# Second products by seven half-size products, for chunks 2 and 3 of the first block and for the second block

## The chip, the cores and the metric

The kernel runs on one core of a Trainium2 chip. The metric is the device time of one execution in microseconds; the median of three runs of the kernel before is 205.09 us (204.23 to 205.53). A second, profiled execution gives the trace that the text reads.

## What is computed

A retention layer (linear attention with a decay per head), then a feed-forward layer with a squared relu. Four batches of 768 tokens, 8 heads of 64, so x has 3072 rows of 512; the feed-forward layer goes 512 to 2048 to 512.

```
state = gamma[h] * state + outer(k[t], v[t])     # per batch and head, over t
y[t]  = q[t] @ state / sqrt(64)
x     = y, heads side by side                    # 3072 x 512
h     = maximum(x @ w_in, 0)                     # 3072 x 2048, "first products"
out   = (h * h) @ w_out                          # 3072 x 512,  "second products"
```

## The kernel before

**Chunks and blocks.** The 3072 tokens are 24 chunks of 128. `BLOCKS` puts four chunks in the first block and two in each of ten others. The feed-forward layer works block by block; the attention of later chunks is threaded between its pieces, so that TensorE always has work.

**Pieces and places.** The order of each engine is written out by hand. `ffn_pieces(tb)` is a generator that issues one piece of a block's feed-forward work per step; after each piece a counter n goes up and `before(n)` issues what `put(place, ...)` has registered for that place, and then the squares that are due. Engines take their instructions in that order and wait only for data and buffers. The first block has pieces 5 to 16 (first products of 12 of the 16 rows of blocks of h; four are done earlier) and 17 to 32 (second products). The second block has pieces 33 to 40 (first products, one per chunk and quarter) and 41 to 48 (second products); the third 49 to 56 and 57 to 64. Attention steps of chunk m are registered by `attend` (chunks 4 to 7) and `attend2` (from 8): scaling of q, k and v, transposes, scores with a mask, state, outputs.

**First products** (L826): `w_in` is the stationary operand, x the moving one; ScalarE takes the relu (L835), VectorE, or ScalarE where so marked, the square in place (L804, L806).

**Second products, plain** (L1022): for a chunk of 128 tokens, 16 matmuls of 512 columns, h the stationary operand, `w_out` the moving one. ScalarE copies the sum out (L1032), SP stores it (L1034). In the first block the four chunks go together, a quarter g of `w_out` at a time: four matmuls per piece, each quarter of `w_out` used by four pieces.

**Second products, seven half products** (L860, in blocks that `SEVEN` names, from the third on): two chunks of tokens, the even and odd blocks of h, and the two halves of the output columns make 2x2 matrices, which are multiplied with seven products instead of eight (Winograd's form of Strassen's scheme). Each product is 8 matmuls of 256 columns. VectorE makes four sums of h (`s1` = a21 + a22, `s2` = s1 - a11, `s3` = a11 - a21 in place of a21, `s4` = a12 - s2; `first_sums` makes the first two in halves) and, after the products, `u`, `v` and three output sums with operands in PSUM (all L856). The four differences of `w_out` (`t1` to `t4`, `sum_w_out`, L319) are made once, for the two halves of `w_out` apart. The last product is put off into the next block (`kept`).

**Buffers and queues.** The first and second products share four PSUM buffers (`ps_f`); the transposes use one (`ps_tp`), the scores one (`ps_st`). `spare` is a tile of the pool of h that the prologue uses for scores. The second half of `w_out`'s quarters come by GpSimd's DMA queue (`load_w_out`, L170, places 6, 8, 11, 14, with a cast on the way); all other loads and the stores are issued by SP in order. `cast_k2` (L688) and the copies of L705 are GpSimd's work for chunks from 8 on, `transpose_k2` (L711) a DMA transpose of what L688 wrote. `pack_constants` and `zero_off_diagonal` (L358) prepare constants and zeros for that later form of attention.

## Time and profile before

| | us |
|---|---|
| median of three runs | 205.09 |
| the profiled execution, its own time | 204.37 |
| its span, first to last instruction | 202.5 |
| granted TensorE clock over the span | 1.00 |
| second products of the first block begin | 30.92 |
| first products of the second block begin | 47.63 |
| first products of the third block begin | 65.29 |
| second products of the third block begin | 73.58 |
| a later block of two chunks, start to start (104.78 to 119.74) | 14.96 |

Times inside the span are counted from its start. A row of the table of groups reads: line, engine, operation, written tile from read tiles, shapes, number of instructions; then busy time in total and the mean of one in ns; then the idle time of the engine just before them and what ended it. A row of a timeline reads: start, length, engine, line, operation, and in brackets the idle time before it and who ended that. Matmuls of a run overlap in the pipeline, so the length of a run divided by its number is less than the duration that one matmul shows.

The engines over three later stretches, one of them in the steady state (columns: stretch, its length, then busy time and number of instructions of PE, PEld, DVE, ACT and POOL, granted clock, DMA share, GB/s):

```profile
43.00:48.00 5.00, 4.95 (x51) 3.31 (x51) 3.84 (x7) 4.08 (x8) 0.61 (x1) 1.00 1.09 267
73.60:80.50 6.90, 6.88 (x103) 6.08 (x100) 5.81 (x11) 4.11 (x10) 2.32 (x4) 1.00 0.76 140
104.60:119.60 15.00, 15.00 (x190) 13.57 (x188) 12.34 (x25) 10.45 (x22) 5.50 (x8) 1.00 0.97 203
```

### The profile page before, as it was taken

The page shows a single profiled execution, that of the slowest core. Times are in us where ns is not written, and L with a number is a line of the kernel's source. Part 1 is how long each engine was busy: PE and PEld are TensorE (multiplying, and loading weights), DVE is VectorE, ACT ScalarE, POOL GpSimd, SP SyncE. Part 2 cuts the span into 40 slices and gives each one's busy share as a digit, 9 for nine tenths or more (in the row PEclk, how much of TensorE's full clock was granted, in tenths as well). Part 3 has the DMA queues.
Part 4 walks back from the last instruction along what each step waited for, and adds up shares of the span by engine and source line. Part 5 has one row for each costly group of instructions (what it writes and reads, how often), then busy time and mean ns, then how long its engine had stood idle before and what let it go on. Part 6 is the DMA issues. An engine that isn't in the chain of part 4 may idle for free.

```text
span 202.5 us, 5744 instructions
## 1 busy us (share of the span) xinstructions
PE 195.7 (97%) x2321; PEld 160.1 (79%) x2327; DVE 151.2 (75%) x309; ACT 127.6 (63%) x258; POOL 68.0 (34%) x131
## 2 busy tenths in 40 slices
PE   5899999999999999999999999999999999999993
PEld 1478444558965998988989999999889899999883
DVE  3986768268597888788798798798797797485374
ACT  8764872348853766782784785783775776763730
POOL 8693711311330552282225225252225225100000
PEclk9999999999999999999999999999999999999999
DMA  5999999999979478979979998979998254300202
GB/s 169 356 375 398 338 195 197 260 233 320 236 160 262 125 159 156 202 204 223 171 214 164 214 208 203 226 182 227 212 157 200 107 105 49 111 3 0 107 0 104
DMA packets 92250, 38.12 MB, mean 188 GB/s; under 512 B 68544, under 2 KB 88256, under 8 KB 92224
## 3 DMA queue, kind: packets, MB, share of 16 engines
q1 hardware_dynamic: 90112, 35.66, 72.3%
q0 software_dynamic: 2112, 2.10, 6.2%
q8 instruction: 18, 0.29, 0.6%
q14 instruction: 8, 0.07, 0.1%
HBM read 27.26 MB, written 6.29 MB: 166 GB/s over the span
## 4 chain that ended last, share of the span: by engine, by line
PE 89%; DVE 4%; DMA 2%; ACT 2%; issue 1%; DVEq 0%
PE psf L826 40%; PE psf L860 18%; PE psf L1022 10%; PE tp L860 7%; DMA qn<-in_q_dram 2%; PE y L783 2%; PE st L727 2%; PE y L776 2%; PE c_ps L754 2%; DVE h L806 1%; PE c_ps L627 1%; PE st L430 1%; PE y L506 1%; ACT h L835 1%; PE y L342 1%
## 5 line engine op out<-in xcount | busy, mean ns | idle before, releaser
L826 PE MATMUL psf<-xt,w_in_bf 128*128 128x256 bf16 (+2 forms) x879 | 92.2, 259 | 0.2 <-issue 0.2
L826 PEld LDWEIGHTS <-w_in_bf 128*128 128x128 bf16 x880 | 71.2, 98 | 11.4
L835 ACT ACTIVATE h<-psf 128x512 bf16<-128x512 f32 x96 | 56.1, 594 | 20.1 <-PE psf L826 18.5
L806 DVE TENSOR_TENSOR h<-h 128x512 bf16<-128x512 bf16 x80 | 35.6, 460 | 19.2 <-ACT h L835 18.8
L688 POOL CAST ks_bdp<-stage 64x512 bf16<-64x512 f32 x32 | 24.5, 767 | 38.7 <-issue 30.7
L705 POOL COPY v_bd<-v 64x512 bf16<-64x512 bf16 x32 | 20.6, 643 | 42.0 <-DVE v L697 36.7
L860 PEld LDWEIGHTS <-h 128*128 128x128 bf16 x288 | 26.3, 98 | 3.8 <-DVE h L806 1.0
L1022 PE MATMUL psf<-w_out_bf,h 128*128 128x512 bf16 x91 | 21.9, 379 | 0.4 <-issue 0.2
L860 PE MATMUL tp<-w_out_bf,h 128*128 128x256 bf16 x136 | 19.4, 273 | 0.2 <-DVE h L806 0.2
L860 PE MATMUL psf<-w_sum,h 128*128 128x256 bf16 x136 | 19.1, 273 | 0.0
L860 PE MATMUL psf<-w_sum,k_bd 128*128 128x256 bf16 x144 | 17.9, 273 | 0.0
L361 DVE TENSOR_TENSOR qs<-qn,qf 128x512 bf16<-128x512 f32 x20 | 16.3, 824 | 0.0
L1022 PEld LDWEIGHTS <-h 128*128 128x128 bf16 x96 | 8.9, 98 | 9.0
L860 PEld LDWEIGHTS <-k_bd 128*128 128x128 bf16 x144 | 13.7, 98 | 1.5
L763 ACT ACTIVATE s_bd<-c_ps 64x256 bf16<-64x256 f32 x29 | 10.7, 370 | 6.5 <-PE c_ps L754 6.5
L856 DVE TENSOR_TENSOR osb<-psf,u 128x256 f32<-128x256 f32 x26 | 10.3, 421 | 6.1 <-PE psf L860 5.8
L856 DVE TENSOR_TENSOR u<-psf,u 128x256 f32<-128x256 f32 x18 | 7.6, 423 | 8.9 <-PE psf L860 8.7
L697 DVE TENSOR_TENSOR v<-stage,kf 128x512 bf16<-128x512 f32 x16 | 12.5, 783 | 0.0
L764 ACT ACTIVATE s_bd<-c_ps 64x256 bf16<-64x256 f32 x29 | 11.0, 378 | 0.4
L734 DVE TENSOR_TENSOR pt<-st,cmask 128x512 bf16<-128x512 f32 x16 | 11.0, 687 | 0.1
L856 DVE TENSOR_TENSOR k_bd<-h 128x512 bf16<-128x512 bf16 x18 | 10.7, 597 | 0.3
L896 ACT ACTIVATE osb<-tp 128x256 f32<-128x256 f32 x8 | 3.1, 384 | 12.2 <-PE tp L860 12.2
(133 smaller groups left out, 262.4 us busy)
## 6 DMA issues: line engine op xcount, KB each, us to landing
qn<-in_q_dram SPq DMA_DIRECT2D x12, 512.0 KB, 4.9
out_dram<-osb SPq DMA_DIRECT2D x23, 256.0 KB, 2.4
stage<-in_k_dram SPq DMA_DIRECT2D x32, 96.0 KB, 3.4
stage<-in_v_dram SPq DMA_DIRECT2D x32, 96.0 KB, 3.5
stage<-in_moe_w_in_dram SPq DMA_DIRECT2D x4, 512.0 KB, 7.1
stage<-in_moe_w_in_dram SPq DMA_DIRECT2D x2, 1024.0 KB, 10.2
w_out_bf<-in_moe_w_out_dram POOLq DMA_DIRECT2D x4, 512.0 KB, 10.3
kn<-in_k_dram SPq DMA_DIRECT2D x6, 256.0 KB, 6.0
```

The lines of the kernel that those rows point to most:

```text
L361: engine.tensor_tensor(out=out, in0=by, in1=table[:, :, None].to_broadcast([P, H, D]), op=ALU.mult)
L688: nc.gpsimd.tensor_copy(ks[rows, :, hh, :].rearrange("s (u p) d -> s u p d", u=2), kn[rows])
L697: nc.vector.tensor_tensor(out=v2.rearrange("s (u p) d -> s u p d", u=2), in0=vn, in1=kf2[:, i, :, :, None].to_broadcast([P, 2, NPAIR, D]), ...
L705: nc.gpsimd.tensor_copy(v_bd[rows, :, hh, :], v2[rows])
L734: nc.vector.tensor_tensor(out=pt[:], in0=st[:], in1=cmask2.rearrange("s r t -> s (r t)")[:, None, :].to_broadcast([P, 2 * NPAIR, C // 2]), ...
L764: nc.scalar.activation(s_bd[halves[1], :, 1, :], c[halves[1]], AF.Copy)
L806: nc.vector.tensor_mul(hv, hv, hv)
L826: nc.tensor.matmul(hp, lhsT=w_in_bf[g][:, cb, fq * 128 : (fq + 1) * 128], rhs=xts[tb][:, cb, cols], start=(cb == 0), stop=(cb == NCB - 1),)
L835: nc.scalar.activation(hv, hp[:], AF.Relu)
L856: nc.vector.tensor_tensor(out=out, in0=in0, in1=in1, op=op)
L860: nc.tensor.matmul(to, lhsT=left[:, j], rhs=right(j) if callable(right) else right[:, j], start=(start and j == 0), stop=(stop and j == NF ...
L1022: nc.tensor.matmul(op[:], lhsT=h_of(tb, f)[:, 0, j * C : (j + 1) * C], rhs=w_out_bf[g][:, fq, cols], start=(f == 0), stop=(f == NFB - 1),)
```

## The change

Chunks 2 and 3 of the first block, and the second block, get their second products as seven half products. Chunks 0 and 1 keep the plain form.

In the first block the 16 pieces of second products are rewritten (`last_of_first`). Pieces 17 to 22, 25 and 26 each hold two of the 16 steps of chunks 0 and 1 together (four matmuls of 512) and one matmul of 256 of the half product `pa`; a quarter of `w_out` is so used up by two pieces. The other pieces hold the remaining products in halves, the last one is put off into piece 34. `pa` and `pe` share one PSUM buffer, `pd` and `pb` another. The sums `s1`, `s2` and `s4` lie in `spare`; `first_sums` are issued at places 11 and 17, `s3` and `s4` at 22.

In the second block `SEVEN` now applies. Its `s1`, `s2` and `s4` get a tile of the pool of h; `s4` is made on GpSimd.

Around it: the differences of `w_out` move from places 25, 31 and 48 to 20, 23 and 27; chunk 4's scaling of q from 21 to 13 and 15, its other steps up to four places earlier; chunks 5 and 7 move by up to three places; the transposed k of chunk 7 uses the scores' PSUM buffer. Three things leave VectorE: the zeros of `zero_off_diagonal` and the scaling of q for chunk 8 go to GpSimd, and the square of one piece of the second block goes to ScalarE.

```diff
-SEVEN = range(2, 11)
+SEVEN = range(1, 11)
...
     def zero_off_diagonal(t, hh):
-        nc.vector.memset(t[halves[hh], :, 1 - hh, :], 0.0)
+        nc.gpsimd.memset(t[halves[hh], :, 1 - hh, :], 0.0)
...
+        if tb == 1:
+            room = hpool.tile([P, 4096], BF16, name="h2").rearrange("e (n j t) -> e n j t", n=4, t=C)
+            s1, s2, s4 = (room[:, n] for n in range(3))
...
-            add(s4, a12, s2, ALU.subtract)
+            add(s4, a12, s2, ALU.subtract, nc.gpsimd if tb == 1 else nc.vector)
...
+    def last_of_first():
...
+        def first_sums(x):
+            add(s1[x], a21[x], a22[x])
+            add(s2[x], s1[x], a11[x], ALU.subtract)
+
+        def last_sums():
+            for x in range(2):
+                add(s3[x], a11[x], a21[x], ALU.subtract)
+            for x in range(2):
+                add(s4[x], a12[x], s2[x], ALU.subtract)
+
+        def second_products():
+            ops = [ps_f.tile([P, DM], FP32, name="psf") for _ in range(2)]
+            pa, pe, pd, pb = (
+                t[:, n * HN : (n + 1) * HN]
+                for t in [ps_f.tile([P, DM], FP32, name="psf") for _ in range(2)]
+                for n in range(2)
+            )
...
+            def plain(j):
+                for f in (2 * j, 2 * j + 1):
+                    for c, op in enumerate(ops):
+                        nc.tensor.matmul(
+                            op[:],
+                            lhsT=h_of(0, f)[:, 0, c * C : (c + 1) * C],
+                            rhs=w_out_bf[f // FPQ][:, f % FPQ, :],
+                            start=(f == 0),
+                            stop=(f == NFB - 1),
+                        )
+                product(pa, a11, b(0, 0), (j,))
+
+            lo, hi = range(0, 4), range(4, 8)
+            for j in range(6):
+                plain(j)
+                yield
+            product(pd, s1, t1, lo)
+            product(pb, s2, t2, lo, False)
+            yield
+            product(pe, a22, t4, lo, False)
+            yield
+            plain(6)
+            yield
+            plain(7)
+            nc.scalar.activation(a[:], pa, AF.Copy)
+            for c, op in enumerate(ops):
+                osb = opool.tile([P, DM], FP32, name="osb")
+                nc.scalar.activation(osb[:], op[:], AF.Copy)
+                nc.sync.dma_start(out[c * C : (c + 1) * C], osb[:])
+            yield
+            product(pa, a12, b(1, 0), lo, False)
+            product(pa, a12, b(1, 0), hi, False)
+            nc.scalar.activation(oa[:, 0:HN], pa, AF.Copy)
+            yield
+            product(pd, s1, t1, hi)
+            yield
+            product(pb, s2, t2, hi)
+            add(u[:], pb, a[:])
+            yield
+            product(pe, a22, t4, hi)
+            yield
+            product(pb, s3, t3, lo, False)
+            yield
+            product(pb, s3, t3, hi, False)
+            add(v[:], pb, a[:])
+            add(ob[:, HN:DM], pd, v[:])
+            add(ob[:, 0:HN], pe, v[:])
+
+            def last_product():
+                product(pd, s4, b(1, 1), range(8), False)
+                add(oa[:, HN:DM], pd, u[:])
...
-            relu(h_of(tb, g * FPQ, (g + 1) * FPQ)[:, :, cols], open_ps.pop((tb, g, c)))
+            relu(h_of(tb, g * FPQ, (g + 1) * FPQ)[:, :, cols], open_ps.pop((tb, g, c)), (tb, c, g) == (1, 1, 2))
...
         if tb == 0:
+            first_sums, last_sums, second_products = last_of_first()
+            put(11, first_sums, 0)
+            put(17, first_sums, 1)
+            put(22, last_sums)
...
+            yield from second_products()
+            return
...
                     first_unit(tb, g, c)
+                    if c * NQ + g in (1, 2, 3) and kept:
+                        next(kept[0])
+                    if c * NQ + g == 4:
+                        kept.clear()
...
-            put(scaled, scale_q, m, 1)
+            put(scaled + 2 if m == 4 else scaled, scale_q, m, 1)
             put(places[0], transpose_q, m)
-        put(places[0], scale_kv, m)
-        put(places[1], transpose_k, m)
+        put(18 if m == 4 else places[0], scale_kv, m)
+        put(places[1], transpose_k, m, *((ps_st, "st") if m == 7 else (ps_tp, "tp")))
...
-            put(q_at, scale_q, m, 0)
-            put(q_at + 1, scale_q, m, 1)
+            on = nc.gpsimd if m == PACK_FROM else nc.vector
+            put(q_at, scale_q, m, 0, on)
+            put(q_at + 1, scale_q, m, 1, on)
...
-    for half, at_places in enumerate(((25, 25, 25, 25), (31, 31, 48, 48))):
+    for half, at_places in enumerate(((20, 20, 20, 20), (23, 23, 27, 27))):
...
-    attend(4, 21, (23, 25, 27, 29, 31))
-    attend(5, None, (28, 30, 31, 32, 34))
+    attend(4, 13, (21, 22, 24, 26, 29))
+    attend(5, None, (25, 28, 30, 32, 34))
     attend(6, 31, (33, 35, 37, 39, 42))
-    attend(7, None, (38, 42, 44, 46, 49))
+    attend(7, None, (36, 40, 43, 45, 48))
```

More of the change, by code (lines that the diff above doesn't have):

```diff
@@ L853, in seven_products, with add @@
         )
-        def add(out, in0, in1, op=ALU.add):
-            nc.vector.tensor_tensor(out=out, in0=in0, in1=in1, op=op)
+        def add(out, in0, in1, op=ALU.add, engine=nc.vector):
+            engine.tensor_tensor(out=out, in0=in0, in1=in1, op=op)
         def product(to, left, right, js, start, stop):
@@ L1034, in store @@
             nc.sync.dma_start(out[r0 : r0 + C, cols], osb[:, cols])
-        together = nch if tb == 0 else 1
-        for j0 in range(0, nch, together):
-            ops = [ps_f.tile([P, DM], FP32, name="psf") for _ in range(together)]
+        for j in range(nch):
+            op = ps_f.tile([P, DM], FP32, name="psf")
             for g in range(NQ):
-                for j, op in enumerate(ops):
-                    second(op, j0 + j, g)
-                    if g == NQ - 1:
-                        store(op, j0 + j)
-                    yield
+                second(op, j, g)
+                if g == NQ - 1:
+                    store(op, j)
+                yield
     tp, st, f = (ps_tp, "tp"), (ps_st, "st"), (ps_f, "psf")
```

39 lines of the change are left out of this document (added).

## The prediction

> **What bounds the kernel now.** I read the page first (busy shares, then the chain that ended last), next the table of windows over the stretch that the change touches, then TensorE's, VectorE's and GpSimd's timelines there, and last the landings of the `w_out` loads. The page and its table of groups:
>
> ```profile
> span 202.5 us, 5744 instructions
> PE 195.7 (97%) x2321; PEld 160.1 (79%) x2327; DVE 151.2 (75%) x309; ACT 127.6 (63%) x258; POOL 68.0 (34%) x131
> PE 89%; DVE 4%; DMA 2%; ACT 2%; issue 1%; DVEq 0%
> ```
>
> TensorE is the bound: it is hardly ever idle and carries 89% of the chain. So work taken from it counts in full, and so does each new wait of it. The windows of the stretch (columns: PE, PEld, DVE, ACT, POOL busy, granted clock, DMA share, GB/s):
>
> ```profile
> 31.00:37.00 6.00, 5.95 (x29) 2.70 (x29) 5.45 (x9) 0.60 (x1) 1.87 (x12) 1.00 1.22 197
> 37.00:43.00 6.00, 5.95 (x40) 3.20 (x40) 1.29 (x2) 2.21 (x3) 1.09 (x3) 1.00 1.12 266
> 53.00:57.00 4.00, 4.00 (x76) 3.85 (x74) 2.94 (x7) 2.86 (x6) 1.65 (x1) 1.00 0.83 187
> 61.00:65.30 4.30, 4.14 (x33) 2.23 (x33) 3.33 (x8) 0.97 (x2) 0.00 (x0) 1.00 1.05 269
> ```
>
> VectorE has room (1.29 of 6 us in one window), the DMA engines have none until about 48 us. TensorE's second products, as the chain of waits and the timeline give them, start here:
>
> ```profile
> 30.92 6.21 PE L1022 MATMUL psf<-w_out_bf,h 128*128 128x512 bf16 x27
> 37.57 1.73 PE psf L1022 x8
> 77.49 0.87 PE psf L860 x8
> ```
>
> In the chain eight 512-wide matmuls take 1.73 us (0.216 each) and eight 256-wide ones 0.87 us (0.109 each). The 379 and 273 ns of the table of groups hold the pipeline's tail and overlap, so I don't add those.
>
> **The change, part by part.** A pair of chunks cost 32 x 0.216 = 6.9 us of second products and costs 56 x 0.109 = 6.1: 0.8 less for chunks 2 and 3, 0.8 less for the second block, 1.6 in all. That is the whole possible gain, apart from TensorE's gaps. From 30.92 to 47.63 (first of the second block) its work is 13.8 + 2.7 of attention = 16.5 of 16.7 us, and from there to 65.29 17.4 of 17.7: 0.4 of gaps in all. I now walk TensorE's new order with these durations.
>
> *First block.* Pieces 17 to 22 each hold two steps of both plain chunks and one of the half product, 4 x 0.216 + 0.109 = 0.97 us. Group 2 of `w_out` is now needed by the fifth piece, at 30.92 + 4 x 0.97 = 34.80; before, by the ninth (37.8). It lands later than that:
>
> ```profile
> 24.66 1.48 POOL L170 DMA_DIRECT2D w_out_bf<-in_moe_w_out_dram  x2
> w_out_bf<-in_moe_w_out_dram POOLq DMA_DIRECT2D x1, 512.0 KB, 11.1
> ```
>
> 24.66 + 11.1 = 35.76 us. Nothing that the change moves is issued before it, so TensorE waits 0.96 us. Group 3 (issued about 25.4, slowest landing 13.8: 39.2) is needed only at 40.4 and costs nothing. Then the transposes of chunk 4 follow each other with one piece between them instead of two: those of k need the PSUM buffer that ScalarE empties with the L397 copy, 1.02 us. From the first transpose that is free at 0.61 + 0.04 + 1.02 + 0.05 = 1.72 us and TensorE is there at 0.45 + 0.97 = 1.42: wait 0.30. The first scores need both L411 copies (1.21) with only 1.3 us of products ahead: 0.14. The product that goes on accumulating in `pa` waits for its copy (0.38, row L884) behind 0.44 us of scores and state: 0.15; two more of 0.05. Sum of new waits 0.96 + 0.30 + 0.14 + 0.15 + 0.10 = 1.65, against 0.8 saved and 0.2 of gaps that are gone: the first block ends 0.6 us later, counting its last product, which now lies in the second block.
>
> *Second block.* 0.8 of work and 0.2 of gaps less, so 1.0 earlier if nothing new stops TensorE. VectorE gets 8 sums of 0.42 and 5 output adds of 0.42 for the first block, 4 sums of 0.42, one of 0.68 and 5 output adds for the second (10.0 us), and loses ten memsets (2.5), two scalings of q (1.3) and one square (0.4): +5.8 us against 11.2 us idle between 31 and 73.6 (31.4 busy, summed over the windows). In its order the `w_sum` differences of the second half now stand ahead of the masks of chunk 4 and wait for group 3 till 39.2; mask and k scaling of chunks 4 and 5 queue behind them, done at 41.3 and 41.9 where TensorE asks at 42.4 and 44.3, so that wait is hidden. The deadlines after that, by the same walk: the second mask of chunk 6 ends at 57.1 (asked at 57.45), the last square of the block at 58.9 (59.2), the second half of `s1` at 59.4 (60.3), the first mask of chunk 7 at 61.8 (62.25). They hold, by only 0.3 to 0.9 us; an undisturbed VectorE costs nothing. ScalarE's added square (0.63, row L804) lies ahead of the last relu, with copies only behind it: nothing. SP's stores are the same bytes; two of them move ahead of v loads that are needed only at 65: nothing.
>
> *GpSimd* takes ten memsets (0.52 for 64x512, row L298), two scalings of q for chunk 8 and the add `s4`. For these two-input operations the only row is this one:
>
> ```profile
> L559 POOL TENSOR_TENSOR ks_bdp<-kn,kfp 128x512 bf16<-128x512 f32 x2 | 2.8, 1395 | 1.7 <-DMA kn<-in_k_dram 1.7
> ```
>
> So 1.4 us per scaling, 2.5 to 3.1 for `s4` (its two instances, 1.24 and 1.55, doubled). `s4` is used in the third block, behind `s2` by over 5 us: hidden. But behind it in GpSimd's queue stand a memset and the casts of chunk 8's keys (1.3 to 1.7), then their DMA transpose (3.1 to 3.8 to landing): from `s2` at 59.8 this gives 67.9 to 69.6, and TensorE asks at 69.3. I take 0, bounds 0 to 0.3. The scalings run at about 52.7 to 56.5, when VectorE has 1.2 us to spare (5.7 us of work between 51.6 and the block's last relu at 58.5). The two engines hinder each other:
>
> ```profile
> 55.35 1.87 POOL L688 CAST ks_bdp<-stage 64x512 bf16<-64x512 f32 x1 [3.13 <-DMA stage<-in_k_dram]
> 67.36 1.09 DVE L361 TENSOR_TENSOR qs<-qn,qf 128x512 bf16<-128x512 f32 x1
> 69.13 1.09 DVE L361 TENSOR_TENSOR qs<-qn,qf 128x512 bf16<-128x512 f32 x1
> 72.13 1.17 DVE L806 TENSOR_TENSOR h<-h 128x512 bf16<-128x512 bf16 x2
> ```
>
> A cast that takes 0.61 elsewhere took 1.87 while VectorE worked without a pause, and VectorE's operations lost about 1.1 us over each 3 us of GpSimd's (0.36 per us) at 66.6 to 69.7 and 72.3 to 75.4. So 2.8 us of scalings cost VectorE 1.0, within its 1.2; at worst both hold it for their whole 1.4, 2.8 - 1.2 = 1.6 on TensorE. I take 0.2, near the first, as VectorE mostly went ahead when it was busy.
>
> Sum: +0.6 - 1.0 + 0.2 = -0.2 us on the span of 202.5, so 204.2 for the profiled execution (204.37). That one lies 0.7 below the median of the runs, 205.09; the median becomes 204.9.
>
> **Rivals.** *Slower: GpSimd holds VectorE.* Its three new two-input instructions block VectorE for their full length. At the scalings this costs up to 1.6 (above). At `s4`: if it starts before VectorE's `s3`, which becomes ready at the same moment, `s3` ends 2.5 late, so the mask of chunk 7 ends at 63.6 where TensorE asks at 62.25: 1.4. Together -0.4 + 3.0 = +2.6, 207.7; it decides from 1.2 us of VectorE delay before 57 us, or from `s4` starting first. For it: the 1.09 and 1.17 above. Against: the 1.87, where GpSimd was the one that waited; and `s3` follows `s2` on its own engine while `s4` waits for a semaphore. The Trainium skill, "SBUF — State Buffer", section "Who interferes with whom", says that a VectorE instruction with two SBUF inputs and a GpSimd instruction that reads SBUF exclude each other for a whole instruction, first come first served. By that rule the memsets and the masks and output adds, which read PSUM, would not be touched, and only `s3`, the squares and the k scaling would be; the rows above agree so far, but none shows an instruction of GpSimd's that is as long as these.
>
> *Faster: the waits of the first block don't come.* If group 2 is there in time, -0.2 - 0.96 gives 203.9; without the small ones too, -0.2 - 1.65 gives 203.2. For: landings of one kind differ by microseconds (7.1 to 13.8). Against: the queue ahead of group 2 is untouched, and at a DMA share of 1.2 it can't come sooner.
>
> *The key transpose of chunk 8 is late:* GpSimd's chain above at its slow end with VectorE late as well, +0.3 to +1, 205.2 to 205.9. *The half products are no cheaper:* the chain's 0.87 per eight, already through seven products per block, speaks against it; it would give 204.9 + 1.6 = 206.5.
>
> **How the numbers follow.** Forecast 204.9 (its own range 204.2 to 205.8): 0.52. GpSimd holds VectorE, 205.9 to 207.7: 0.24. No waits, 203.0 to 203.9: 0.18. Late key transpose or dearer products: 0.06. One per cent, about what a measurement of this kernel can tell from no change, is 2.05 us: faster than 203.04 takes nearly everything of the gain and the gaps, 0.04; slower than 207.14 takes the upper part of GpSimd's case and a little of the last, 0.16; within, 0.80. The range 203.5 to 206.8 leaves out the lower end of the fast case and the upper of GpSimd's, about 0.1 each.
>
> **What would show it.** In the new profile: TensorE idle about 1 us at 34.8 before the second products, with a DMA on `w_out` as releaser (if not, the fast case); idle 0.3 before L404 at about 38; the third block's first product near 64.9 (65.3 before); VectorE's squares at 53 to 57 not over 0.8 us each (if over 1 us with TensorE idle before chunk 7's transposes, GpSimd's case); `s3` at 0.7 us just ahead of `s4` on GpSimd. The prediction is wrong if TensorE's idle time in 31 to 74 us adds up to more than 4 us or to less than 0.8.

## The result, and the profile after

The changed kernel takes 206.37 us (median of 8 runs, 205.12 to 207.85) beside 204.84 for the kernel before on the same chip (8 runs, 204.23 to 205.54): ratio 1.0075, 95% interval 1.0049 to 1.0101, so 1.5 us slower (1.0 to 2.1). Twelve later runs gave the same ratio (run after_timed below).

The page of its profile, the lines that answer to the three of before:

```profile
span 204.2 us, 5869 instructions
PE 195.8 (96%) x2372; PEld 165.2 (81%) x2375; DVE 158.5 (78%) x319; ACT 127.3 (62%) x259; POOL 76.0 (37%) x144
PE 79%; DVE 11%; DMA 4%; ACT 4%; issue 1%; DVEq 0%; POOLq 0%
```

TensorE's busy time is no smaller (195.8 after 195.7), and the chain now runs over VectorE and DMAs for 15% instead of 6%. The 1.6 us that the half products save can't be read from the busy time, in which the pipeline's tail at every stop counts as busy (a stop of 1.05 us below stands as 0.89 idle); starts of stages show more. Besides the two profiles at hand I took a second of each kernel:

| start of, in us | before | before, 2nd | changed | changed, 2nd |
|---|---|---|---|---|
| second products, first block | 30.92 | 31.19 | 31.95 | 30.93 |
| second block | 47.63 | 47.90 | 47.90 | 47.84 |
| third block | 65.29 | 65.56 | 66.03 | 65.98 |
| its second products | 73.58 | 73.84 | 74.52 | 74.47 |
| second products, seventh block | 134.54 | 134.82 | 136.31 | 135.62 |
| span | 202.5 | 202.7 | 204.2 | 203.6 |

The first row is the trap of this case. TensorE's instructions up to there are the same in both kernels, and still it lies at 30.9, 31.2 or 31.95 in their executions (the kernel before with one added subtraction far behind it, below, also has 31.96). The traces show what goes with it, though no run varied it: how soon TensorE reaches its full speed. The first line is of the profile before, the second of the changed kernel's first:

```profile
6.46 0.38 PE L342 MATMUL y<-ident 128*128 128x512 bf16 x1
6.51 0.63 PE L342 MATMUL y<-ident 128*128 128x512 bf16 x1
```

Over all twenty profiles of this case, the matmuls of the prologue get short (0.38 us for 512 columns, 0.22 for 128) at 5.4 to 6.87 us where the second products begin by 31.19, and at 6.95 to 8.18 us where they begin at 31.95 or 31.96. In the changed kernel the late start makes hardly any difference: what follows waits for the load of `w_out`, and the third block's second products begin at 74.5 either way. In the kernel before it moves everything: 73.58 with the early start, 74.61 with the late one. So the change costs 0.9 us up to that point when the prologue is early, and gains 0.1 when it is late. The second profile of the changed kernel, with the early start, is the one to compare with the profile before. Its windows over the stretch of the change (columns as before):

```profile
31.00:37.00 6.00, 5.06 (x28) 2.53 (x28) 5.53 (x12) 0.60 (x1) 1.15 (x1) 1.00 1.22 197
37.00:43.00 6.00, 5.78 (x51) 3.82 (x49) 3.83 (x8) 2.64 (x5) 2.26 (x14) 1.00 1.09 259
53.00:57.00 4.00, 3.69 (x67) 3.57 (x64) 3.66 (x4) 3.33 (x7) 3.82 (x6) 1.00 0.91 253
61.00:65.30 4.30, 4.30 (x52) 3.80 (x50) 2.83 (x5) 1.36 (x3) 3.99 (x4) 1.00 0.89 202
```

TensorE lost 0.94 of 6 us in the first window (0.05 before) and 0.31 of 4 in the third (none before), where GpSimd is busy for 3.82 instead of 1.65. Its timeline there, same profile:

```profile
34.71 0.27 PE L987 MATMUL psf<-w_out_bf,h 128*128 128x256 bf16 x1
35.87 1.02 PE L1020 MATMUL psf<-w_out_bf,h 128*128 128x512 bf16 x4 [0.89 <-DMA w_out_bf<-in_moe_w_out_dram]
...
38.15 0.27 PE L987 MATMUL psf<-w_out_bf,h 128*128 128x256 bf16 x1
38.56 0.38 PE L404 MATMUL tp<-ident,ks 128*128 128x128 bf16 x4
...
45.52 0.28 PE L506 MATMUL y<-pt,v_bd 128*128 128x128 bf16 x2
46.00 0.61 PE L987 MATMUL psf<-w_sum,h 128*128 128x256 bf16 x4 [0.20 <-DVE w_sum L319]
...
54.74 1.95 PE L826 MATMUL psf<-xt,w_in_bf 128*128 128x128 bf16 x32
57.14 0.38 PE L430 MATMUL st<-qT,k_bd 128*128 128x128 bf16 x4 [0.45 <-DVE pt L437]
```

Four stops, read by starts (a bracket leaves out the pipeline's tail): group 2 of `w_out` 1.05 us (35.87 less 34.71 + 0.11), the PSUM buffer of the transposes 0.30 (38.56 less 38.15 + 0.11), the half product with `t4` 0.36, the mask of chunk 6 0.61 (57.14 less 54.74 + 1.79). The third comes from VectorE's order, in which the differences for `t4` stand behind the copy of the state:

```profile
44.21 0.43 DVE L483 CAST s_bd<-c_ps 64x256 bf16<-64x256 f32 x1 [0.73 <-ACT s_bd L481]
44.65 0.69 DVE L319 TENSOR_TENSOR w_sum<-w_out_bf 128x1024 bf16<-128x1024 bf16 x1
45.26 0.68 DVE L319 TENSOR_TENSOR w_sum<-w_out_bf,w_sum 128x1024 bf16<-128x1024 bf16 x1
```

The last comes from VectorE's squares:

```profile
53.34 1.36 DVE L806 TENSOR_TENSOR h<-h 128x512 bf16<-128x512 bf16 x1 [0.48 <-ACT h L835]
54.62 0.68 DVE L361 TENSOR_TENSOR ks<-kn,kf 128x512 bf16<-128x512 f32 x1
55.23 1.26 DVE L806 TENSOR_TENSOR h<-h 128x512 bf16<-128x512 bf16 x1
```

and from what GpSimd does meanwhile:

```profile
53.38 1.04 POOL L361 TENSOR_TENSOR qs<-qn,qf 128x512 bf16<-128x512 f32 x1
54.48 0.52 POOL L358 MEMSET ks_bdp<- 64x512 bf16 x1
55.08 1.13 POOL L361 TENSOR_TENSOR qs<-qn,qf 128x512 bf16<-128x512 f32 x1
```

A square of 0.42 takes 1.36 and 1.26: it stands for about as long as GpSimd's scaling runs. The scaling of k at 54.62, with two inputs in SBUF as well, keeps its 0.68 beside a memset. That is the rule of the Trainium skill, "SBUF — State Buffer", section "Who interferes with whom": GpSimd's reads hold VectorE's two-input instructions for a whole instruction, its writes alone don't. This trace agrees with both halves.

The first profile of the changed kernel shows a further loss that neither profile of before has: TensorE waits for key transposes, as at 128.38, 0.6 us in all.

```profile
128.38 0.41 PE L727 MATMUL st<-qT,kT 128*128 128x64 bf16 x8 [0.28 <-DMA kT<-ks_bdp]
```

### The profile page after: what moved, and what is told of

The parts are those of the page before. It is cut to its first block, busy times and chain, and to the rows that moved or that the text cites. A ratio compares the mean times of both kernels' runs of the same rounds, so it can differ in the third digit from the quotient of the medians.

```text
span 204.2 us, 5869 instructions
## 1 busy us (share of the span) xinstructions
PE 195.8 (96%) x2372; PEld 165.2 (81%) x2375; DVE 158.5 (78%) x319; ACT 127.3 (62%) x259; POOL 76.0 (37%) x144
## 4 chain that ended last, share of the span: by engine, by line
PE 79%; DVE 11%; DMA 4%; ACT 4%; issue 1%; DVEq 0%; POOLq 0%
PE psf L826 35%; PE psf L863 19%; PE tp L863 8%; PE psf L1020 3%; DVE h L806 3%; DMA kT<-ks_bdp 2%; PE st L727 2%; DMA qn<-in_q_dram 2%; PE y L783 2%; PE c_ps L754 1%; PE y L776 1%; PE psf L987 1%; ACT h L835 1%; PE y L342 1%; DVE pt L437 1%
## 5 line engine op out<-in xcount | busy, mean ns | idle before, releaser
L806 DVE TENSOR_TENSOR h<-h 128x512 bf16<-128x512 bf16 x79 | 38.1, 501 | 13.9 <-ACT h L835 13.6
L688 POOL CAST ks_bdp<-stage 64x512 bf16<-64x512 f32 x32 | 23.1, 722 | 36.1 <-issue 19.7
L863 PEld LDWEIGHTS <-h 128*128 128x128 bf16 x344 | 31.4, 98 | 4.6 <-DVE h L806 1.3
L863 PE MATMUL psf<-w_sum,h 128*128 128x256 bf16 x168 | 23.4, 273 | 0.0
L863 PE MATMUL tp<-w_out_bf,h 128*128 128x256 bf16 x152 | 21.7, 273 | 0.5 <-DVE h L806 0.5
L859 DVE TENSOR_TENSOR osb<-psf,u 128x256 f32<-128x256 f32 x29 | 11.4, 420 | 6.7 <-PE psf L863 6.3
L859 DVE TENSOR_TENSOR u<-psf,u 128x256 f32<-128x256 f32 x20 | 8.4, 422 | 9.7 <-PE psf L863 9.5
L361 DVE TENSOR_TENSOR qs<-qn,qf 128x512 bf16<-128x512 f32 x18 | 14.4, 803 | 0.9 <-DMA qn<-in_q_dram 0.6
L804 ACT ACTIVATE h<-h 128x512 bf16<-128x512 bf16 x17 | 10.7, 629 | 0.5
L377 POOL CAST v_bd<-vn 128x512 bf16<-128x512 f32 x4 | 3.1, 777 | 20.8 <-DMA vn<-in_v_dram 12.9
```

The source lines that it names most:

```text
L361: engine.tensor_tensor(out=out, in0=by, in1=table[:, :, None].to_broadcast([P, H, D]), op=ALU.mult)
L688: nc.gpsimd.tensor_copy(ks[rows, :, hh, :].rearrange("s (u p) d -> s u p d", u=2), kn[rows])
L806: nc.vector.tensor_mul(hv, hv, hv)
L859: engine.tensor_tensor(out=out, in0=in0, in1=in1, op=op)
L863: nc.tensor.matmul(to, lhsT=left[:, j], rhs=right(j) if callable(right) else right[:, j], start=(start and j == 0), stop=(stop and j == NF ...
```

## The experiments

Times are medians; a ratio is to the kernel before on the same chip, with its 95% interval.

**Second profiles of both kernels.** No edit.

> The kernel before, unchanged, a second profile. Theory CHANCE (the prologue's start-up differs from execution to execution): its second products begin at another time than 30.92 us, anywhere in 30.9 to 32. Theory CHANGE (the later start is the change's doing): again within 0.1 us of 30.92. Both expect 17.66 us from there to the third block's second products less its start: 42.66 +- 0.2, and no wait for a key transpose (L711) of over 0.2 us behind 74 us.

> The changed kernel, unchanged, a second profile. CHANCE: second products begin before 31.95 us, and then TensorE's wait for group 2 of w_out, hidden in the first profile, shows: if they begin at 31.0, about 0.9 us idle ahead of the fifth piece of second products. CHANGE: again 31.95 +- 0.1 and no such wait. In both, VectorE's squares beside GpSimd's two scalings of q take over 1.2 us each again. Theory LATER (the queue of SP lags in the steady state): waits for key transposes of 0.2 us or more again behind 90 us; if they were chance, none.

Before: second products at 31.19, 42.65 us to the third block's, no late transpose. Changed: 30.93, and the wait for group 2 that the first profile hid, 0.89. CHANCE holds for the prologue. Late key transposes cost 0.18 this time (0.64 in the first profile, 0.00 in a third).

**Each block alone.** In the first, `SEVEN` from 2 on, chunk 7's steps, the scalings of q and the square as before; in the second, the first block, its attention places and chunk 4's scaling as before (the last two differences of `w_out` at place 34 instead of 48, since the second block uses them).

```diff
# first_block_alone
-SEVEN = range(1, 11)
+SEVEN = range(2, 11)
-            on = nc.gpsimd if m == PACK_FROM else nc.vector
+            on = nc.vector
-    attend(7, None, (36, 40, 43, 45, 48))
+    attend(7, None, (38, 42, 44, 46, 49))
...
# second_block_alone
-            yield from second_products()
-            return
-    for half, at_places in enumerate(((20, 20, 20, 20), (23, 23, 27, 27))):
+    for half, at_places in enumerate(((25, 25, 25, 25), (31, 31, 34, 34))):
...
```

> Only the first block in the new form (with its moved attention steps and the zeros on GpSimd); second block plain, scaling of q for chunk 8 on VectorE. If the cost sits in the first block (wait for group 2, the PSUM buffers): 0.4 to 1.0 us slower than before, second products of the first block 16.9 to 17.5 us long to the second block's start (16.7 before). If the cost is the second block's (GpSimd beside VectorE): within 0.3 us of before. If what counts is a later stage that any shift upsets: 0.7 us slower with waits for key transposes behind 90 us.

> Only the second block in the new form (its sums, s4 and the scaling of q for chunk 8 on GpSimd, the square on ScalarE, chunk 7's steps); the first block plain. If the first block is to blame: 0.3 to 1.0 us faster than before (its 0.8 of products and 0.2 of gaps, less GpSimd's 0.2 to 0.6). If GpSimd is to blame: 0 to 0.8 us slower, with squares of over 1.2 us and TensorE idle 0.5 us or more in the second block. If a later stage that any shift upsets: gain up to the third block, given back behind 80 us.

First block alone: 205.70 beside 204.61, 1.0039 (1.0022 to 1.0055). Its start was 31.19; it lies 0.83 us behind the second profile of before at the third block, and no late transposes follow. Second block alone: 204.56, 0.9992 (0.9973 to 1.0012), 0.2 behind at the third block's second products: 0.8 saved, and given back in two stops of 0.5, before the scores of chunk 6 (ScalarE's `k_bd`) and at the mask. So the first block is what costs, the second doesn't pay, and 0.8 and 0.0 leave 0.7 of the 1.5 for the two together.

**The waits of the first block.** In half_products_first, three half products go ahead of the pieces that need group 2, and `w_sum` and chunk 4's steps move with them; in sums_of_w_earlier only the last two differences move.

```diff
# half_products_first
-            for j in range(6):
+            for j in range(4):
                 plain(j)
                 yield
             product(pd, s1, t1, lo)
             product(pb, s2, t2, lo, False)
             yield
             product(pe, a22, t4, lo, False)
             yield
+            for j in range(4, 6):
+                plain(j)
+                yield
             plain(6)
...
-    for half, at_places in enumerate(((20, 20, 20, 20), (23, 23, 27, 27))):
+    for half, at_places in enumerate(((17, 17, 17, 17), (23, 23, 26, 26))):
-    attend(4, 13, (21, 22, 24, 26, 29))
+    attend(4, 13, (21, 23, 25, 27, 30))
# sums_of_w_earlier
-    for half, at_places in enumerate(((20, 20, 20, 20), (23, 23, 27, 27))):
+    for half, at_places in enumerate(((20, 20, 20, 20), (23, 23, 26, 26))):
```

> The changed kernel with three half products (pd, pb, pe, first halves) ahead of the pieces that need group 2 of w_out, the differences of w_out for them at place 17, and chunk 4's steps one place further apart. Theory GROUP 2 (the wait for the load, 0.9 to 1.05 us when the prologue is in time): gone, with the 0.3 before L404 and the wait for t4 as well, so that the second products of the first block take 15.2 to 15.6 us to the second block's start instead of 16.9: 1.0 to 1.6 faster than the changed kernel, between 0.5 slower and 0.2 faster than before. Rival (the differences of w_out are late instead, as VectorE has no room): second products wait for w_sum at 34.8 to 36 us, gain under 0.5.

> The changed kernel with the last two differences of w_out at place 26 instead of 27, so ahead of the state's copy in VectorE's order. Theory: the wait of 0.2 to 0.36 us before the half product with t4 (46.0 us) goes, and the second block starts 0.3 earlier. Rival: the state's copy comes later and the outputs of chunk 4 wait in its place; no gain.

sums_of_w_earlier: the wait is gone, the second block starts at 47.62 instead of 47.90 with the same late prologue (31.95). Its one run took 206.41, as key transposes cost 1.5 us later on. half_products_first: 205.61, 1.0041 (1.0018 to 1.0064), 0.7 faster than the changed kernel by the two ratios, where 1.0 to 1.6 was expected. Its profile had the late prologue, where there was no wait for group 2 to remove, and gained 0.1 up to the third block's second products (0.5 was lost at a key transpose at 77 us); the same order with the early one (next run) ends the first block 0.69 earlier. The wait didn't go whole: `w_out`'s group 3 and the copy of `pa` became the next stops, 0.5 each in that run.

**GpSimd's hold on VectorE.** Chunk 8's scalings of q back on VectorE, alone and with the order above.

```diff
-            on = nc.gpsimd if m == PACK_FROM else nc.vector
+            on = nc.vector
```

> The changed kernel with chunk 8's two scalings of q back on VectorE. Theory EXCLUSION (a scaling on GpSimd holds VectorE's square for its whole length): both squares back to 0.42, the wait of L430 for the mask of chunk 6 (0.45) gone, the third block's second products 0.5 to 0.7 us earlier from the start of the second block's, so 0.5 to 0.7 faster than the changed kernel (0.4 to 1.0 slower than before). Rival (VectorE is too full in that stretch anyway): the same time as the changed kernel, the wait still there.

> The two together: half products ahead of group 2, scalings of q on VectorE. If the two costs are separate they add up: 1.5 to 2.2 faster than the changed kernel, 203.2 to 204.2 us and 0.5 to 1.3 faster than before. If one hides the other: no faster than the better of the two alone.

qs_on_vector: the squares take 0.42 again, so EXCLUSION is right about its cause, and TensorE gains nothing: the two scalings of 0.6 us now stand ahead of the mask in VectorE's own order, and the wait has moved by one instruction.

```profile
57.08 1.07 PE L826 MATMUL psf<-xt,w_in_bf 128*128 128x128 bf16 x16
58.59 0.38 PE L404 MATMUL st<-ident,ks 128*128 128x128 bf16 x4 [0.45 <-DVE pt L437]
```

Third block's second products at 74.45 (74.47 before the edit). It took 206.96, 1.0116 (1.0086 to 1.0146), with 1.6 us of late transposes. both_mended: third block's second products at 73.78, 0.69 earlier, all of it from the first block; 205.87, 1.0056 (1.0032 to 1.0081), against 203.2 to 204.2 expected, so the two costs did not add up; the profiled execution took 204.46.

**The late key transposes: GpSimd's queue?** My first theory was that `s4` on GpSimd puts off the casts of chunk 8's keys, and SP's queue with them. Three edits: `s4` on VectorE; the casts at place 43 instead of 44, ahead of `s4`; and, in the kernel before, a subtraction about as long as `s4` (2.12 us beside 2.44) in its place.

```diff
# s4_on_vector
-            add(s4, a12, s2, ALU.subtract, nc.gpsimd if tb == 1 else nc.vector)
+            add(s4, a12, s2, ALU.subtract)
# casts_ahead_of_s4
-        8: (37, 41, 44, 46, 48), 9: (0, 0, 49, 51, 53), 10: (50, 54, 55, 57, 60), 11: (0, 0, 60, 63, 68)
+        8: (37, 41, 43, 46, 48), 9: (0, 0, 49, 51, 53), 10: (50, 54, 55, 57, 60), 11: (0, 0, 60, 63, 68)
# before_with_a_subtraction_on_gpsimd
+    def work_on_gpsimd():
+        room = hpool.tile([P, 4096], BF16, name="h2").rearrange("e (n j t) -> e n j t", n=4, t=C)
+        h = h2s[1][0].rearrange("e (j k) (c t) -> e k c j t", k=2, c=2)
+        nc.gpsimd.tensor_tensor(out=room[:, 2], in0=h[:, 1, 0], in1=h[:, 1, 1], op=ALU.subtract)
+    put(43, work_on_gpsimd)
```

> The changed kernel with the second block's s4 on VectorE. Theory QUEUE (GpSimd's s4 puts off the casts of chunk 8's keys, their DMA transpose waits at the head of SP's queue, the loads behind it come later, and SP, which issues without a pause from there on, never makes it up, so key transposes come late some 40 us on): L711 for chunk 8 issued at 62.5 to 64.2 instead of 65.3 to 65.7, the one of chunk 14 by 107.5 (108.4 to 110.2 in the changed kernel), no wait of L727 for a key transpose; 0.4 to 1.0 us faster than the changed kernel. Theory CHANCE (late transposes come and go with the DMA engines' load): the waits of L727 as before, 0.2 to 2 us.

> The changed kernel with only the order of GpSimd changed: the casts of chunk 8's keys ahead of s4. QUEUE: the same as with s4 on VectorE, so L711 for chunk 8 issued before 64.2, no late key transposes behind 100 us, 0.4 to 1.0 faster than the changed kernel. If instead s4's own length or its hold on VectorE matters: no gain here, and a gain with s4 on VectorE.

> The kernel before, with one useless subtraction of 128x1024 on GpSimd, as long as s4 and in its place, ahead of the casts of chunk 8's keys; its result is not used. QUEUE: L711 for chunk 8 issued at 64.5 to 65.5 (62.7 and 63.4 before), key transposes of chunks 14 to 17 about 1 us later than before, waits of L727 of 0 to 1 us, so 0.1 to 0.8 us slower than before with nothing else changed up to 73 us. CHANCE: the time of before, within 0.2 us.

QUEUE fell three times. The transpose of chunk 8 was issued at 62.1 and 62.8 as expected, yet those of chunk 14 at 110.0 and 110.6, with TensorE 1.0 and 1.2 us late in the sixth and seventh blocks: 206.03, 1.0046 (1.0025 to 1.0067) and 206.62, 1.0058 (1.0034 to 1.0082). The kernel before with the subtraction issued chunk 8's at 65.2, chunk 14's at 107.1, and took 205.06, 1.0001 (0.9980 to 1.0022). What these profiles do show is where SP loses the time, in the loads between the transposes of chunks 12 and 14 (s4_on_vector, SP's timeline):

```profile
90.49 1.25 SPq L711 DMA_TRANSPOSE kT<-ks_bdp  x1
92.48 6.13 SPq L145 DMA_DIRECT2D stage<-in_k_dram  x7
...
103.37 3.15 SPq L145 DMA_DIRECT2D stage<-in_v_dram  x2
...
110.01 1.27 SPq L711 DMA_TRANSPOSE kT<-ks_bdp  x1
```

The same seven loads took 4.65 and the same two 1.29 in the profile before. SP makes no pause between these two transposes in any of the twenty profiles, so what it loses there it does not get back at once. Ahead of them it does: at chunk 10's transpose the changed kernel's three profiles are 3.2 to 4.2 us behind the third block's second products (2.1 and 2.2 before), but chunk 12's, the first line above, comes only 0.08 us behind the fourth block's (90.41). In all profiles but two it is 0.06 to 0.7 behind there (0.24 and 0.29 before), and 1.96 and 2.17 only in the changed kernel's first and in qs_on_vector. So in most of them the lag is not carried over from the stretch of the change: it arises anew from chunk 12's transpose to chunk 14's. That takes 16.7 to 17.0 us in the four profiles that have the second block plain (before_with_a_store_in_eight, 17.4, aside), and 17.2 to 19.5 in the fifteen that have it in half products.

**The late key transposes: SP's lag.** Three runs: the changed kernel again; the four stores of the first two blocks' half products on ScalarE's queue; the kernel before with one store of the second block issued in eight parts.

```diff
# stores_by_scalar, seven_products; in last_of_first nc.scalar for both
-                        nc.sync.dma_start(out[r0 + C : r0 + 2 * C], ob[:])
+                        queue = nc.scalar if tb == 1 else nc.sync
+                        queue.dma_start(out[r0 + C : r0 + 2 * C], ob[:])
                         yield
-                        nc.sync.dma_start(out[r0 : r0 + C], oa[:])
+                        queue.dma_start(out[r0 : r0 + C], oa[:])
# before_with_a_store_in_eight
-            nc.sync.dma_start(out[r0 : r0 + C, cols], osb[:, cols])
+            n = 8 if (tb, j) == (1, 1) else 1
+            for i in range(0, C, C // n):
+                nc.sync.dma_start(out[r0 + i : r0 + i + C // n, cols], osb[i : i + C // n, cols])
```

> The changed kernel, unchanged, with its runs on the same chip as the next three, so that they can be compared with it: 205.3 to 206.6 us. Theory LAG (SP's queue runs further behind TensorE from the third block on, and key transposes land too late once it is about 2.9 us behind): in this profile too L711 for chunk 14 is issued 2.9 us or more behind the fifth block's first second product, and L727 waits.

> The changed kernel with the four stores of the half products of the first two blocks issued by ScalarE's DMA queue, so that SP issues four DMAs fewer between 50 and 73 us. LAG: L711 for chunk 10 issued 0.5 to 1.5 us earlier against the third block's second products (3.2 to 4.3 behind in the changed kernel, 2.2 before), the one of chunk 14 less than 2.9 behind the fifth block's, no wait of L727 for key transposes, and 0.3 to 1.0 us faster than the changed kernel in the same runs. Rival LOAD (the transposes themselves take longer, SP's place in time doesn't matter): the same waits of 0.2 to 2 us, the same time.

> The kernel before, with the store of the second chunk of the second block issued by SP as eight of 16 rows instead of one of 128: the same bytes, seven more issues on SP at 66 us. LAG: SP falls 1 to 2.5 us further behind, L711 of chunk 14 is issued 2.9 us or more behind the fifth block's second products, L727 waits for key transposes at 112 to 130 us, and the kernel is 0.2 to 1.5 us slower than before, though nothing is changed on the other engines. LOAD: the time of before, within 0.2 us.

The kernel before with seven more issues on SP took 208.30 by the median of six runs; the ratio, without the longest of them (209.6), is 1.0152 (1.0104 to 1.0200). Nothing else in it was changed. SP's timeline and then TensorE's:

```profile
66.13 4.62 SPq L1036 DMA_DIRECT2D out_dram<-osb  x8
70.79 2.33 SPq L145 DMA_DIRECT2D stage<-in_k_dram  x3
73.24 1.28 SPq L711 DMA_TRANSPOSE kT<-ks_bdp  x1
```

```profile
76.67 0.41 PE L727 MATMUL st<-qT,kT 128*128 128x64 bf16 x8 [1.03 <-DMA kT<-ks_bdp]
83.21 0.41 PE L727 MATMUL st<-qT,kT 128*128 128x64 bf16 x8 [0.62 <-DMA kT<-ks_bdp]
```

The store's eight issues take 4.62 us instead of 0.34, the transpose behind them is issued at 73.24 instead of 69.7, and TensorE stands still for it. The waits came some 35 us sooner than I had expected, but LAG's mechanism is shown: a delay on SP alone reaches TensorE.

after_timed: 206.44, 1.0075 (1.0046 to 1.0103); its profiled execution, 205.11, was its fastest, with chunk 14's transpose 2.4 us behind the fifth block's second products and no wait, against my "2.9 or more". stores_by_scalar: 205.80, 1.0048 (1.0023 to 1.0073), lag 2.2, no wait in the profile; 0.6 faster than the changed kernel, but the intervals overlap. Over the profiles, the lag of chunk 14's transpose (how long after the fifth block's first second product SP issues it) beside TensorE's delay in the first products of the sixth and seventh blocks (their length above 8.79 us each, in steady state):

| profile | lag | delay |
|---|---|---|
| before, twice; first_block_alone; before with a subtraction | 1.4 to 2.0 | 0.0 |
| both_mended, stores_by_scalar, after_timed, second_block_alone | 2.2 to 2.6 | 0.0 |
| all_mended and its second and third form (below) | 2.4 to 2.8 | 0.0 |
| after_again, half_products_first | 2.9, 3.0 | 0.2, 0.0 |
| after | 3.9 | 0.6 |
| all_mended_3_stores_by_scalar | 4.0 | 1.1 |
| s4_on_vector, casts_ahead_of_s4, sums_of_w_earlier, qs_on_vector | 4.3 to 4.4 | 1.0 to 1.6 |

(The kernel with the store in eight parts, which waits 30 us earlier, is left out.) Up to a lag of 2.8 nothing waits, from 3.9 on every profile does.

**A version that beats both?** all_mended adds to both_mended: the casts ahead of `s4`, the scalings of q at places 39 and 40, and `pd`'s second half ahead of the product that waits for the copy of `pa`. The second puts the scalings at 41 and 42; the third also moves `s4` to VectorE, behind the last mask; the fourth has the stores on ScalarE's queue as well.

```diff
# all_mended, to both_mended
-        8: (37, 41, 44, 46, 48), 9: (0, 0, 49, 51, 53), 10: (50, 54, 55, 57, 60), 11: (0, 0, 60, 63, 68)
+        8: (39, 41, 43, 46, 48), 9: (0, 0, 49, 51, 53), 10: (50, 54, 55, 57, 60), 11: (0, 0, 60, 63, 68)
+            product(pd, s1, t1, hi)
+            yield
             product(pa, a12, b(1, 0), lo, False)
             product(pa, a12, b(1, 0), hi, False)
             nc.scalar.activation(oa[:, 0:HN], pa, AF.Copy)
             yield
-            product(pd, s1, t1, hi)
-            yield
# all_mended_2, to all_mended
-        8: (39, 41, 43, 46, 48), 9: (0, 0, 49, 51, 53), 10: (50, 54, 55, 57, 60), 11: (0, 0, 60, 63, 68)
+        8: (41, 43, 43, 46, 48), 9: (0, 0, 49, 51, 53), 10: (50, 54, 55, 57, 60), 11: (0, 0, 60, 63, 68)
# all_mended_3, to all_mended_2
-            add(s4, a12, s2, ALU.subtract, nc.gpsimd if tb == 1 else nc.vector)
+            if tb != 1:
+                add(s4, a12, s2, ALU.subtract)
...
+                    if tb == 1:
+                        add(s4, a12, s2, ALU.subtract)
                     add(v[:], pb[:], a[:])
```

> The half products ahead of group 2 and the scalings of q on VectorE as in the run of both, and besides the casts ahead of s4, the scalings of q behind the masks of chunk 6 (wait of 0.45 for the mask), and the second half of pd ahead of the product that waits for the copy of pa (0.47). QUEUE and the priced waits: span 201.5 to 202.2, time 203.0 to 204.0, all runs close together; 0.6 to 1.5 us faster than before. If the waits only move: 204.5 or more.

> The run all_mended with chunk 8's scalings of q two places later, behind the last square of the second block, for which TensorE waited 0.7 us there. If that wait was all that stood there: span 201.2 to 201.6 in a profile whose prologue is in time, 0.5 to 0.8 us faster than all_mended and 0.7 to 1.4 us faster than before. LAG adds that some runs may lose 0.2 to 1 us to late key transposes.

> all_mended_2 with the second block's s4 on VectorE, behind the last mask of that stretch, so that nothing on GpSimd holds VectorE there. HOLD (in all_mended_2 s4 on GpSimd started first and VectorE's two scalings took 3.21 instead of 1.28 us, TensorE idle 1.8 us and its granted clock 0.72 behind that): the two scalings together at 1.3 us, that wait under 0.2 us, granted clock 1.00 in 62 to 68 us, the third block's second products at 72.3 to 72.8 us when the prologue is in time. LAG: SP does not come earlier by as much as TensorE does, so L711 of chunk 14 is 2.8 to 3.6 us behind the fifth block's second products and some runs lose 0.2 to 0.8 us there: 203.3 to 204.6 us, 0.2 to 1.4 faster than before.

> all_mended_3 with the four stores of the half products of the first two blocks on ScalarE's queue. LAG: 0.1 to 0.6 us faster than all_mended_3, L711 of chunk 14 under 2.9 us behind, runs closer together, 203.0 to 204.2 us. LOAD: the same as all_mended_3.

all_mended: 204.52, 0.9983 (0.9960 to 1.0006); third block's second products at 73.14, with 0.7 us lost where a square stands behind a scaling. all_mended_2 was to remove that, and was slower: 206.72, 1.0082 (1.0056 to 1.0109). Now the scalings met `s4`. VectorE, GpSimd and TensorE in its profile:

```profile
58.88 3.21 DVE L361 TENSOR_TENSOR qs<-qn,qf 128x512 bf16<-128x512 f32 x2
```

```profile
59.12 2.43 POOL L859 TENSOR_TENSOR h<-h,h 128x1024 bf16<-128x1024 bf16 x1 [2.40 <-DVE h L859]
```

```profile
63.47 0.38 PE L430 MATMUL st<-qT,k_bd 128*128 128x128 bf16 x4 [1.79 <-DVE pt L437]
```

Two scalings of 1.28 took 3.21, and TensorE stood idle for 1.8 us. all_mended_3 confirms HOLD: 1.28 for the two scalings, no such wait, third block's second products at 72.40, 1.2 earlier than before with the same prologue. Its time is still 205.19, 1.0001 (0.9971 to 1.0031), from 203.68 (the quickest of all kernels here) to 206.53; the last form 205.29, 1.0016 (0.9988 to 1.0044), its profile with a lag of 4.0 us and 1.1 of delay in the sixth and seventh blocks: no help from the stores there. So no version is faster than the kernel before clear of the noise (all_mended comes nearest); a gain of 1.2 us on TensorE at 73 us is there and is not kept.

## Why the prediction was wrong

The forecast was -0.2, the result +1.5. The range, 203.5 to 206.8, holds the median.

*Right.* Group 2 landed at 35.87 (35.76 priced) and cost 1.05 (0.96); L404's buffer 0.30 (0.30); the copy of `pa` 0.17 (0.15); the scores 0.11 (0.14). The products are cheaper by the 0.8 us per pair of chunks: second_block_alone shows it, its two stops taken off. `s3` went ahead of `s4` (0.68 us at 60.9) and the key transpose of chunk 8 made nobody wait by itself.

*First block, +0.6 forecast, +1.07 measured* (17.78 us with the last product against 16.71, early prologue). The step that failed is "that wait is hidden": I looked there at masks and scalings behind `w_sum`, and never asked when the last two differences are done. They wait on VectorE behind the copy of the state, which waits 0.73 for ScalarE, and TensorE waits 0.36 for `t4`; sums_of_w_earlier takes that away.

*Second block, -0.8 forecast, -0.18 measured.* The step "So 2.8 us of scalings cost VectorE 1.0, within its 1.2", from which came "I take 0.2", took the smaller of two prices. GpSimd's scaling is shorter than priced (1.04 and 1.13) and its hold is nearly whole: 1.78 us of VectorE for 2.17 of GpSimd, 0.8 per us and not 0.36. Less the 1.2 that VectorE had to spare, this gives about the 0.6 at the mask. The 0.2 of gaps that I had booked as gone is the rest. qs_on_vector shows that this is not a loss of the move to GpSimd: in VectorE's order at the same places the scalings cost as much. My marker of 64.9 for the third block was itself wrong: it left out that the second block's last product (0.87) goes behind it and the outputs of chunk 7 (0.67) ahead of it. The second products are the better mark: 73.4 forecast, 74.47 measured.

*Base.* I took the runs of before to be alike but for noise, and set the forecast against one profile with the early start. The kernel before begins its second products anywhere from 30.9 to 31.96; the changed one, tied to the load, has no use for the early start. With the shares of after_timed's 28 runs of before (10 of them above 205.3, taken as late) that makes 0.9 for 18 and -0.1 for 10: +0.5 on the mean up to the third block, where the early profile alone says +0.9.

*Later blocks, 0 forecast, the remaining 1.0 us.* "The key transpose of chunk 8 is late" was priced as TensorE's wait for that one transpose. Nobody waits for that one; the waits come 40 to 60 us later, at transposes from chunk 14 on, which the prediction put at nothing because SP's stores "are the same bytes". They do not come from chunk 8's transpose being late (three runs), and in most profiles SP is in step again at chunk 12's. That a delay on SP reaches TensorE is shown (before_with_a_store_in_eight). That it makes up the 1 us in the unprofiled runs is inferred: the quickest run, 205.11, is the one whose profile has no such wait, the others go up to 207.5, and profiles with a lag of 3.9 or more show 0.6 to 1.6. Why SP takes longer from chunk 12's transpose to chunk 14's when the second block is in half products stays open: not because of `s4` or the casts (three runs), and perhaps in part because of the four stores (one run for, one against).

Of the rivals, GpSimd's was half right (the scalings, 0.6 of up to 1.6), and its other half, `s4` ahead of VectorE's work, came true in all_mended_2, at 1.8 us and more. "No waits in the first block" comes true for group 2 alone when the prologue is late, and then without a gain, as the start itself is 1.0 later; the smaller waits stay.

## What to carry to other kernels

Take two or three profiles of a kernel before reading a difference of half a per cent: one late prologue hid the main wait of this change. When work is made cheaper on the engine that bounds, list the landings it now runs into, and book every in-order queue that runs without a pause (here SP) as an engine with a lag of its own; follow that lag from stage to stage, since here it was made up once and arose again 20 us later. In these traces an operation on GpSimd that reads SBUF holds VectorE's operations with two SBUF inputs for most of its length (1.78 of 2.17 us), and one left on VectorE cost the same where it stood ahead of what TensorE asked next: the place counted, not the engine.

## What was not expected of the hardware

In one profile a wait of 1.8 us cost TensorE as much again afterwards. The windows of all_mended_2 around it (third value from the end: the granted clock):

```profile
62.00:63.00 1.00, 0.00 (x0) 0.00 (x0) 0.97 (x3) 0.00 (x0) 0.13 (x1) 1.00 0.48 118
63.00:64.00 1.00, 0.53 (x12) 0.41 (x11) 0.86 (x3) 0.00 (x0) 0.00 (x0) 1.00 1.05 320
64.00:65.00 1.00, 1.00 (x14) 0.76 (x7) 0.97 (x2) 0.51 (x2) 0.00 (x0) 0.66 1.15 256
65.00:66.00 1.00, 1.00 (x7) 0.70 (x5) 0.05 (x1) 0.25 (x1) 0.00 (x0) 0.50 1.27 266
66.00:67.00 1.00, 1.00 (x10) 0.88 (x9) 0.42 (x1) 0.00 (x0) 0.00 (x0) 0.50 0.88 192
67.00:68.00 1.00, 1.00 (x14) 1.00 (x13) 0.97 (x3) 0.15 (x1) 0.00 (x0) 0.63 0.59 136
```

The clock falls to 0.50 one microsecond after work has begun again and is back at 68: some 3.4 us at half speed (1.7 us of work lost: 0.34 + 0.50 + 0.50 + 0.37) for 1.8 idle. The Trainium skill, "TensorE: Matmul & The Clock Gate", section "What's actually happening", has the half clock and a free-running window of about 3.4 us, and asks for an idle window of that length; the length of the slow stretch agrees, but here, in this one profile, about half as much idle time was enough. The gaps of up to 1.0 us in the other profiles did not lower the clock.
